# Grouped-query attention with a key/value cache: wide scores, block transposes on VectorE, and an eight-way load of 640 wo rows

## The chip, the cores and the metric

The kernel runs on one core of one Trainium2 chip. The metric is the device time of one execution in microseconds (us), lower is better. TensorE (PE; PEld is its weight load), VectorE (DVE), ScalarE (ACT), GpSimd (POOL) and SyncE (SP) run their own instruction queues in order; sixteen DMA engines carry the loads.

## The reference

Batch 8, four query positions, model width 512, 32 query heads over 8 kv heads (four query heads share one), 2048 cached keys, head size 128, all in bf16.

```
q = (x @ wq).reshape(B, Sq, Hq, Dh).transpose(0, 2, 1, 3)
k = repeat(k_cache, 4, axis=1);  v = repeat(v_cache, 4, axis=1)
p = softmax(einsum("bhqd,bhkd->bhqk", q, k) * Dh**-0.5)
o = einsum("bhqk,bhkd->bhqd", p, v)
out = o.transpose(0, 2, 1, 3).reshape(B, Sq, Hq * Dh) @ wo
```

The inputs are 33.6 MB of keys, 33.6 MB of values, 4.2 MB of wq, 4.2 MB of wo and 32 KB of x; the output is 32 KB.

## The kernel before

**Units.** The work is cut into 16 units `(hq, b)`: one batch entry and four kv heads. One unit's keys are one load of 2 MB into a tile of 128 partitions x 64 keys x 128 (32 partitions per kv head), its values another. `kpool` and `vpool` have three buffers each. The projection of x (L164 to L206) is made once, into `q_bd`, which holds the queries in two halves `e` of the head size, zero where the other half stands.

**One unit's steps.** `transpose_part(u, t)` (L143), for t = 0 to 3, turns a quarter of the keys on TensorE, two bf16 at a time as one fp32, through PSUM tiles `kp`; VectorE copies them to `kt`. `scores(u)` (L212) makes 32 matmuls of 256 columns: the 128 rows of `s_ps` are 4 quarters `t` of the keys x 32, and the four kv heads `g` follow each other in the columns. ScalarE takes the exponential head by head (four instructions, each with a sum `l_sb`). `probs_to_keys(u)` (L236) turns the 128x128 blocks of probabilities with 8 TensorE transposes into `pt`, and ScalarE copies the four 32-row bands into `probs`. `norms(u)` (L252) gathers the sums with a matmul against ones and takes the reciprocal; `values(u, half)` (L273) is 32 matmuls a half against the value tile; `finish(u)` scales the result into `oT`.

**The order** is written out by hand (`manual_schedule`, the loop at L323). Iteration n turns the keys of unit n in four parts, and between them makes the scores of unit n-1 and the norms and values of unit n-2. After unit B (half of the heads done), `to_tokens` and `to_wo_rows` (L295, L303) bring the outputs from head order into rows of wo; after the last unit they do it for the other half. `project(p, r0, n)` multiplies by wo: `wo_sb[:, p, r, :]` holds row r of each partition's eight rows of part p, and four parts are summed in `out_ps`.

**The loads** all go through SP's queue in the order of a list: k0, wq, x, k1, then k(u) and v(u-2) in turn; part 0 of wo stands before v14, parts 1 and 2 and four quarters of part 3 come last. `load_ready` issues what the free buffers allow; a load into a buffer that is still read waits at the head of SP's queue. wo takes the place of wq in SBUF (one buffer, tag "w"). Every load but x has 128 partitions as its outermost dimension on both sides; x has 32.

Of the kernel before, what the change touches and what calls it, by code (L numbers as in the profile page):

```python
# [14 lines left out]
def kernel(  # L15
# [18 lines left out]
    G = 4  # L34
# [7 lines left out]
    NP = Hq // HP  # L42
    DH = D // 2
    NU = (Hkv // G) * B
    KB, VB = 3, 3
    scale = float(Dh) ** -0.5
    AX = mybir.AxisListType.X
# [4 lines left out]
    const = ctx.enter_context(tc.tile_pool(name="const", bufs=1))  # L52
# [22 lines left out]
    by_q = const.tile([128, HQ], FP32, name="by_q")  # L75
    oT = [const.tile([128, HP, 2, B, Sq], BF16, name=f"oT{n}") for n in range(2)]
    oP = [const.tile([128, WR, 2, T], BF16, name=f"oP{n}") for n in range(2)]
    nat_sb = const.tile([2 * T, HP * 128], BF16, name="nat_sb")
# [30 lines left out]
    for u in range(2, NU + 2):  # L109
        if u < NU:  # L110
            loads.append(("k", u))
        if u == NU:
            loads.append(("w", 0))
        loads.append(("v", u - 2))
    loads.reverse()

    def load_ready(nk, nv):

        while loads:
            kind, u = loads[-1]  # L120
            if kind == "w":
                load_wo(u, 0, WR)
# [12 lines left out]
    nc.gpsimd.memset(probs[1][:, :, :, :], 0.0)  # L135
    nc.gpsimd.memset(ones[:, :], 1.0)
    nc.vector.tensor_reduce(
        out=by_q[:, :], in_=ident4[:, :].rearrange("p (c q) -> p q c", q=HQ), axis=AX, op=ADD
    )

    kt = {}
# [1 line left out]
    def transpose_part(u, t):  # L143

        k4 = ks[u][:, :, :].rearrange("s c d -> s (c d)").bitcast(FP32)
        kt[(u, t)] = ktpool.tile([128, J, 128, 2], BF16, tag="kt", name="kt")
        for half in range(2):
            kp = psum_k.tile([128, J // 2, 128], FP32, tag="k", name="kp")
            for j in range(J // 2):
                w = (t * J + half * J // 2 + j) * 128  # L150
                nc.tensor.transpose(kp[:, j, :], k4[:, w : w + 128], ident4[:, :])  # L151
            nc.vector.tensor_copy(  # L152
                out=kt[(u, t)][:, half * J // 2 : (half + 1) * J // 2, :, :].rearrange(
                    "k j s e -> k (j s e)"
                ),
                in_=kp[:, :, :].rearrange("k j s -> k (j s)").bitcast(BF16),
            )

# [10 lines left out]
    nc.vector.tensor_copy(out=xT_sb[:, :, :], in_=xtp[:, :, :])  # L169
    q_nats = []  # L170
    for hq in range(Hkv // G):
        psq = psum_s.tile([128, rep * Dh], FP32, tag="s", name="psq")
# [38 lines left out]

    def scores(u):  # L212
        hq, b = units[u]
        s_sbs[u] = small.tile([128, J, G, S], BF16, tag="s_sb", name="s_sb")
        l_sbs[u] = small.tile([128, G], FP32, tag="l_sb", name="l_sb")
        for gg in range(G // 2):
            s_ps = psum_s.tile([128, 2, J, S], FP32, tag="s", name="s_ps")
            for g in range(2 * gg, 2 * gg + 2):
                for e in range(2):
                    for t in range(NT):  # L220
                        nc.tensor.matmul(  # L221
                            s_ps[t * 32 : (t + 1) * 32, g % 2, :, :],
                            lhsT=q_bd[:, hq, e, g, b, :, :],
                            rhs=kt[(u, t)][:, :, g * S : (g + 1) * S, e],
                            start=(e == 0),
                            stop=(e == 1),
                        )
            for g in range(2 * gg, 2 * gg + 2):
                nc.scalar.activation(  # L229
                    out=s_sbs[u][:, :, g, :],  # L230
                    in_=s_ps[:, g % 2, :, :],
                    func=EXP,
                    accum_out=l_sbs[u][:, g : g + 1],
                )

    def probs_to_keys(u):  # L236
        pt = psum_t.tile([128, J, 128], BF16, tag="t", name="pt")
        for j in range(J):
            nc.tensor.transpose(  # L239
                pt[:, j, :], s_sbs[u][:, j, :, :].rearrange("q g s -> q (g s)"), ident[:, :]  # L240
            )
        pr = probs[u % 2]
        for g in range(G):
            rows = slice(g * S, (g + 1) * S)
            nc.scalar.copy(  # L245
                out=pr[rows, :, g, :],
                in_=pt[rows, :, :].rearrange("s j (c q) -> s (j c) q", q=HQ),
            )

    r_sbs = {}  # L250

    def norms(u):  # L252
        by_gq = small.tile([128, G, HQ], FP32, tag="by_gq", name="by_gq")
        nc.vector.tensor_tensor(  # L254
            out=by_gq[:, :, :],
            in0=l_sbs[u][:, :].unsqueeze(2).to_broadcast([128, G, HQ]),
            in1=by_q[:, :].unsqueeze(1).to_broadcast([128, G, HQ]),
            op=MULT,
        )
        l_ps = psum_l.tile([128, NQ], FP32, tag="l", name="l_ps")  # L260
        nc.tensor.matmul(  # L261
            l_ps[:, :],
            lhsT=ones[:, :],
            rhs=by_gq[:, :, :].rearrange("k g q -> k (g q)"),
            start=True,
            stop=True,
        )
        r_sbs[u] = small.tile([128, NQ], FP32, tag="r_sb", name="r_sb")
        nc.vector.reciprocal(r_sbs[u][:, :], l_ps[:, :])  # L269
# [3 lines left out]
    def values(u, half):  # L273
        if half == 0:
            o_pss[u] = psum_o.tile([128, NQ], FP32, tag="o", name="o_ps")
        for i in range(half * C // 2, (half + 1) * C // 2):
            j, t, c = i // 8, i // 2 % 4, i % 2
            nc.tensor.matmul(  # L278
                o_pss[u][:, :],
                lhsT=vs[u][:, 2 * (t * J + j) + c, :],  # L280
                rhs=probs[u % 2][:, i, :, :].rearrange("s g q -> s (g q)"),
                start=(i == 0),
                stop=(i == C - 1),
            )
# [10 lines left out]
    def to_tokens(n):  # L295
        nat = psum_l.tile([2 * T, HP, 128], BF16, tag="l", name="nat")
        for h in range(HP):
            nc.tensor.transpose(
                nat[:, h, :], oT[n][:, h, :, :, :].rearrange("d p b s -> d (p b s)"), ident[:, :]
            )  # L300
        nc.vector.tensor_copy(out=nat_sb[:, :], in_=nat[:, :, :].rearrange("t h d -> t (h d)"))

    def to_wo_rows(n):  # L303
        perm = psum_l.tile([128, WR, 2, T], BF16, tag="l", name="perm")
        by_row = nat_sb[:, :].rearrange("t (q r) -> t r q", r=WR)
        for r in range(WR):
            nc.tensor.transpose(
                perm[:, r, :, :].rearrange("q p t -> q (p t)"), by_row[:, r, :], ident[: 2 * T, : 2 * T]
            )
        nc.vector.tensor_copy(out=oP[n][:, :, :, :], in_=perm[:, :, :, :])  # L310

    def project(p, r0, n):
# [84 lines left out]
```

## Time and profile before

| | |
|---|---|
| time, three runs | 190.15, 190.44, 190.62 us; median 190.44 us |
| profiled execution | the profile gives its span, 188.4 us from the first to the last instruction; the median of the three runs is 2.0 us above that |
| instructions in the span | 5301 |
| busy | PE 140.1 us (74%), PEld 121.5 (65%), DVE 103.5 (55%), ACT 94.4 (50%), POOL 8.2 (4%) |
| read from HBM | 75.53 MB, 401 GB/s over the span |
| TensorE's granted clock, mean | 0.967 |

Busy time is a union of instruction times on an engine. The profile also names, for each idle stretch, what ended it, and follows a chain of such releases back from the last instruction. For each DMA it has packets with their start, duration and size, and the sixteen increments, one per DMA engine, with which a load's semaphore reaches its full count; it does not number the DMA engines.

### The profile page before, as it was taken

What the parts mean: (1) busy time and instruction counts of PE and PEld (TensorE: products, weight loads), DVE (VectorE), ACT (ScalarE), POOL (GpSimd) and SP (SyncE); (2) the same over time, 40 slices, a digit from 0 to 9 for tenths busy, and PEclk for the clock granted to TensorE, in tenths of its full rate; (3) what the DMA queues carried; (4) which work ended last, traced back from release to release, by engine and by line L of the source; (5) the groups of instructions that cost most, each with busy time, mean ns of one, the idle gap of its engine ahead of it and who ended that gap; (6) DMA issues with size and microseconds to landing.
All of it is one profiled execution on the core that took longest, in us unless ns stands there. A gap on an engine that the chain in (4) does not pass through costs nothing.

```text
span 188.4 us, 5301 instructions
## 1 busy us (share of the span) xinstructions
PE 140.1 (74%) x2356; PEld 121.5 (65%) x2356; DVE 103.5 (55%) x189; ACT 94.4 (50%) x200; POOL 8.2 (4%) x11
## 2 busy tenths in 40 slices
PE   0290869797979777777777888879777777776681
PEld 0290357696968766767675878777767677665560
DVE  4082286777776656574747457575747565740120
ACT  2000243958476573646556093919292837468500
POOL 8800000000000000000000000000000000000000
PEclk9999678999999999999999699999999999999997
DMA  6998999999999999999999999999999999999940
GB/s 202 466 445 383 428 421 431 428 411 435 431 402 438 426 431 411 431 435 414 421 438 421 431 418 435 418 424 435 421 418 438 419 428 412 414 445 414 399 184 12
DMA packets 5926, 75.89 MB, mean 403 GB/s; under 512 B 688, under 2 KB 784, under 8 KB 1296
## 3 DMA queue, kind: packets, MB, share of 16 engines
q1 hardware_dynamic: 5856, 75.55, 95.2%
q8 instruction: 18, 0.29, 0.6%
q14 instruction: 4, 0.03, 0.0%
q10 hardware_dynamic: 48, 0.02, 0.0%
HBM read 75.53 MB, written 0.03 MB: 401 GB/s over the span
## 4 chain that ended last, share of the span: by engine, by line
DMA 69%; PE 23%; DVE 4%; ACT 1%; issue 1%; SPq 1%
DMA wo_sb<-in_wo_dram 25%; DMA k_sb<-in_k_cache_dram 21%; DMA v_sb<-in_v_cache_dram 14%; PE kp L151 11%; DMA x_sb<-in_x_dram 9%; PE o_ps L278 4%; PE s_ps L221 3%; DVE kt L152 3%; PE psq L176 2%; PE pt L239 1%; PE l_ps L261 1%; ACT q_bd L201 1%; DVE q_bd L201 0%; ACT q_nat L185 0%; DVE by_gq L254 0%
## 5 line engine op out<-in xcount | busy, mean ns | idle before, releaser
L152 DVE COPY kt<-kp 128x1024 bf16<-128x1024 bf16 x128 | 82.0, 682 | 42.7 <-PE kp L151 42.6
L245 ACT COPY probs<-pt 32x1024 bf16<-32x1024 bf16 x64 | 64.2, 1002 | 58.4 <-PE pt L239 57.2
L151 PE MATMUL kp<-ident,k_sb 128*128 128x128 f32 x512 | 71.5, 286 | 16.9 <-DMA k_sb<-in_k_cache_dram 16.6
L151 PEld LDWEIGHTS kp<-ident,k_sb 128*128 128x128 f32 x512 | 59.0, 148 | 22.3 <-issue 13.2
L278 PE MATMUL o_ps<-probs,v_sb 128*128 128x64 bf16 x1024 | 35.7, 195 | 4.4 <-DMA v_sb<-in_v_cache_dram 4.4
L278 PEld LDWEIGHTS <-v_sb 128*128 128x128 bf16 x1024 | 34.0, 99 | 5.2 <-DMA v_sb<-in_v_cache_dram 5.1
L229 ACT ACTIVATE s_sb<-s_ps 128x256 bf16<-128x256 f32 x64 | 23.6, 383 | 2.2 <-PE s_ps L221 1.9
L221 PE MATMUL s_ps<-kt,q_bd 128*32 128x256 bf16 x512 | 18.6, 286 | 0.0
L261 PE MATMUL l_ps<-by_gq,ones 128*128 128x64 f32 x32 | 6.9, 298 | 15.6 <-DVE by_gq L254 15.6
L261 PEld LDWEIGHTS l_ps<-by_gq,ones 128*128 128x128 f32 x32 | 4.8, 188 | 19.3 <-DVE by_gq L254 17.6
L221 PEld LDWEIGHTS <-q_bd 128*32 128x32 bf16 x512 | 12.7, 97 | 3.7 <-issue 2.6
L269 DVE RECIPROCAL r_sb<-l_ps 128x64 f32<-128x64 f32 x16 | 8.9, 557 | 9.0 <-PE l_ps L261 9.0
L229 ACT ACTIVATION_READ_ACCUMULATOR s_sb<-s_ps 128x1 f32 x64 | 13.2, 206 | 0.0
L288 DVE TENSOR_TENSOR oT<-o_ps,r_sb 128x64 bf16<-128x64 f32 x16 | 3.6, 224 | 16.1 <-PE o_ps L278 16.1
L185 ACT ACTIVATE q_nat<-psq 128x512 bf16<-128x512 f32 x2 | 1.2, 597 | 20.0 <-PE psq L176 20.0
L239 PE MATMUL pt<-ident,s_sb 128*128 128x128 bf16 x128 | 9.8, 219 | 0.3 <-ACT s_sb L229 0.3
L239 PEld LDWEIGHTS <-s_sb 128*128 128x128 bf16 x128 | 8.4, 98 | 0.6 <-ACT s_sb L229 0.5
L315 PE MATMUL out_ps<-wo_sb,oP 128*32 128x256 bf16 x64 | 4.5, 274 | 1.0 <-DMA wo_sb<-in_wo_dram 0.5
L364 ACT CAST out_sb<-out_ps 64x256 bf16<-64x256 f32 x1 | 0.4, 365 | 8.2 <-PE out_ps L315 8.2
L315 PEld LDWEIGHTS <-oP 128*32 128x32 bf16 x64 | 3.0, 96 | 2.0 <-issue 0.9
L176 PE MATMUL psq<-wq_sb,xT_sb 128*32 128x512 bf16 x32 | 3.5, 623 | 0.3 <-DVE xT_sb L169 0.3
L134 POOL MEMSET probs<- 128x4096 bf16 x1 | 3.5, 3511 | 0.0
(27 smaller groups left out, 29.1 us busy)
## 6 DMA issues: line engine op xcount, KB each, us to landing
k_sb<-in_k_cache_dram SPq DMA_DIRECT2D x16, 2048.0 KB, 21.8
v_sb<-in_v_cache_dram SPq DMA_DIRECT2D x16, 2048.0 KB, 25.3
wq_sb<-in_wq_dram SPq DMA_DIRECT2D x1, 4096.0 KB, 17.0
wo_sb<-in_wo_dram SPq DMA_DIRECT2D x3, 1024.0 KB, 23.7
wo_sb<-in_wo_dram SPq DMA_DIRECT2D x4, 256.0 KB, 22.3
x_sb<-in_x_dram SPq DMA_DIRECT2D x1, 32.0 KB, 16.7
out_dram<-out_sb SPq DMA_DIRECT2D x1, 16.0 KB, 1.4
out_dram<-out_sb ACTq DMA_DIRECT2D x1, 16.0 KB, 1.6
```

Of the source, the lines that this page charges most:

```text
L151: nc.tensor.transpose(kp[:, j, :], k4[:, w : w + 128], ident4[:, :])
L152: nc.vector.tensor_copy(out=kt[(u, t)][:, half * J // 2 : (half + 1) * J // 2, :, :].rearrange("k j s e -> k (j s e)"), in_=kp[:, :, :].re ...
L176: nc.tensor.matmul(psq[g * T : (g + 1) * T, :], lhsT=xT_sb[:, r, :], rhs=wq_sb[:, r, c0 : c0 + rep * Dh], start=(r == 0), stop=(r == R - 1),)
L221: nc.tensor.matmul(s_ps[t * 32 : (t + 1) * 32, g % 2, :, :], lhsT=q_bd[:, hq, e, g, b, :, :], rhs=kt[(u, t)][:, :, g * S : (g + 1) * S, e] ...
L229: nc.scalar.activation(out=s_sbs[u][:, :, g, :], in_=s_ps[:, g % 2, :, :], func=EXP, accum_out=l_sbs[u][:, g : g + 1],)
L239: nc.tensor.transpose(pt[:, j, :], s_sbs[u][:, j, :, :].rearrange("q g s -> q (g s)"), ident[:, :])
L245: nc.scalar.copy(out=pr[rows, :, g, :], in_=pt[rows, :, :].rearrange("s j (c q) -> s (j c) q", q=HQ),)
L261: nc.tensor.matmul(l_ps[:, :], lhsT=ones[:, :], rhs=by_gq[:, :, :].rearrange("k g q -> k (g q)"), start=True, stop=True,)
L269: nc.vector.reciprocal(r_sbs[u][:, :], l_ps[:, :])
L278: nc.tensor.matmul(o_pss[u][:, :], lhsT=vs[u][:, 2 * (t * J + j) + c, :], rhs=probs[u % 2][:, i, :, :].rearrange("s g q -> s (g q)"), star ...
L288: nc.vector.tensor_tensor(out=oT[hq][:, :, :, b, :].rearrange("d h p s -> d p h s"), in0=o_pss[u][:, :].rearrange("d (p h s) -> d p h s", ...
L315: nc.tensor.matmul(out_ps[half * T : (half + 1) * T, :], lhsT=oP[p // 2][:, r, p % 2, :], rhs=wo_sb[:, p, r, half * DH : (half + 1) * DH], ...
```

## The change

Six things are changed together.

1. **Scores.** One `s_ps` tile of two PSUM banks for a unit; the 128 rows are now 4 kv heads x 32, and a matmul has 512 columns: 16 matmuls instead of 32. One exponential instruction with one sum replaces four. `kt` holds half of a unit's keys in a tile (three buffers instead of six of half the size).
2. **Probabilities.** The eight TensorE transposes, their PSUM tile and pool go; VectorE turns the scores in 32x32 blocks of 4-byte elements (two bf16 side by side), SBUF to SBUF, and ScalarE's four copies read that tile.
3. **Norms.** A per-partition scalar multiplication replaces the product of two broadcast tensors.
4. **PSUM and SBUF.** `psum_k` has four buffers instead of three, and `psq` moves there. The pool `const` is opened after the pools of the large tiles, and a pad of 384 bytes stands ahead of them: the tiles of wq, wo, k, v and kt now start at multiples of 512 bytes, where they started 192 bytes past one.
5. **wo.** The first 640 rows of part 0 are dealt out so that row `(b * 8 + a) * 5 + r` goes to partition `16 a + b`; they are loaded in two pieces (two and three of the five row slots), after v4 and after v10, with 8 as the source's outermost dimension. The other 384 rows are loaded where all of part 0 was.
6. **The turn into wo rows** follows that deal for half 0 (three copies in `to_tokens`, 16 small matmuls in `to_wo_rows`), and uses matmuls into fp32 in place of transposes into bf16.

```diff
+    XR = 5
...
+    align = ctx.enter_context(tc.tile_pool(name="align", bufs=1))
+    align.tile([128, 192], BF16, name="pad")
...
-    ktpool = ctx.enter_context(tc.tile_pool(name="ktpool", bufs=6))
+    ktpool = ctx.enter_context(tc.tile_pool(name="ktpool", bufs=3))
+    const = ctx.enter_context(tc.tile_pool(name="const", bufs=1))
...
-    psum_k = ctx.enter_context(tc.tile_pool(name="psum_k", bufs=3, space=bass.MemoryType.PSUM))
-    psum_s = ctx.enter_context(tc.tile_pool(name="psum_s", bufs=2, space=bass.MemoryType.PSUM))
-    psum_t = ctx.enter_context(tc.tile_pool(name="psum_t", bufs=1, space=bass.MemoryType.PSUM))
+    psum_k = ctx.enter_context(tc.tile_pool(name="psum_k", bufs=4, space=bass.MemoryType.PSUM))
+    psum_s = ctx.enter_context(tc.tile_pool(name="psum_s", bufs=1, space=bass.MemoryType.PSUM))
...
     def load_wo(p, r0, n):
-        rows = wo[p * HP * 128 : (p + 1) * HP * 128, :].rearrange("(q r) j -> q r j", r=WR)
-        nc.sync.dma_start(wo_sb[:, p, r0 : r0 + n, :], rows[:, r0 : r0 + n, :])
+        rows = wo[p * HP * 128 : (p + 1) * HP * 128, :]
+        if p == 0 and r0 < XR:
+            rows = rows[: 128 * XR, :].rearrange("(b a r) j -> a b r j", a=8, r=XR)
+            nc.sync.dma_start(wo_sb[:, p, r0 : r0 + n, :], rows[:, :, r0 : r0 + n, :])
+        elif p == 0:
...
+            rows = rows[128 * XR :, :].rearrange("(q r) j -> q r j", r=WR - XR)
+            nc.sync.dma_start(wo_sb[:, p, r0:, :], rows)
...
         if u == NU:
-            loads.append(("w", 0))
+            loads.append(("w", (XR, WR - XR)))
         loads.append(("v", u - 2))
+        if u == 6:
+            loads.append(("w", (0, 2)))
+        if u == 12:
+            loads.append(("w", (2, 3)))
...
+        s_ps = psum_s.tile([128, 2, 2 * J, S], FP32, tag="s", name="s_ps")
+        for tp in range(2):
+            for e in range(2):
+                for g in range(G):
+                    nc.tensor.matmul(
+                        s_ps[g * 32 : (g + 1) * 32, tp, :, :],
+                        lhsT=q_bd[:, hq, e, g, b, :, :],
+                        rhs=kt[(u, tp)][:, :, g * S : (g + 1) * S, e],
...
+        nc.scalar.activation(
+            out=s_sbs[u][:, :, :, :].rearrange("q a s j -> q a j s"),
+            in_=s_ps[:, :, :, :].rearrange("q t (a j) s -> q (t a) j s", j=2),
+            func=EXP,
+            accum_out=l_sbs[u][:, :],
+        )
...
-        pt = psum_t.tile([128, J, 128], BF16, tag="t", name="pt")
-        for j in range(J):
-            nc.tensor.transpose(
-                pt[:, j, :], s_sbs[u][:, j, :, :].rearrange("q g s -> q (g s)"), ident[:, :]
-            )
+        p_t = small.tile([128, 2 * J * 2, HQ, 2], BF16, tag="p_t", name="p_t")
+        nc.vector.transpose(
+            p_t[:, :, :, :].rearrange("s x q j -> s (x q j)").bitcast(FP32),
+            s_sbs[u][:, :, :, :].rearrange("q a s j -> q (a s j)").bitcast(FP32),
+        )
...
+        nc.vector.tensor_scalar_mul(
+            out=w_gq[:, :],
+            in0=by_gq[:, :, :].rearrange("k g q -> k (g q)"),
+            scalar1=l_sbs[u][:, 0:1],
+        )
...
-        perm = psum_l.tile([128, WR, 2, T], BF16, tag="l", name="perm")
+        perm = psum_l.tile([128, WR, 2, T], FP32, tag="l", name="perm")
...
+            if n == 0:
+                first = by_few[:, r, :] if r < XR else by_rest[:, r - XR, :]
+                for p, in_ in enumerate([first, by_row[:, r, :]]):
+                    nc.tensor.matmul(
+                        perm[:, r, p, :],
+                        lhsT=in_,
+                        rhs=ident[: 2 * T, p * T : (p + 1) * T],
...
```

More of the change, by code (lines that the diff above doesn't have):

```diff
@@ L50 @@
     assert Dh == 128 and C == 64 and J == 8 and HQ == 16 and NU == 16 and T == 32
-    const = ctx.enter_context(tc.tile_pool(name="const", bufs=1))
+    align = ctx.enter_context(tc.tile_pool(name="align", bufs=1))
+    align.tile([128, 192], BF16, name="pad")
     wpool = ctx.enter_context(tc.tile_pool(name="wpool", bufs=1))
@@ L74 @@
     ones = const.tile([128, 128], FP32, name="ones")
-    by_q = const.tile([128, HQ], FP32, name="by_q")
+    by_gq = const.tile([128, G, HQ], FP32, name="by_gq")
     oT = [const.tile([128, HP, 2, B, Sq], BF16, name=f"oT{n}") for n in range(2)]
@@ L101, in load_wo @@
     def load_wo(p, r0, n):
-        rows = wo[p * HP * 128 : (p + 1) * HP * 128, :].rearrange("(q r) j -> q r j", r=WR)
-        nc.sync.dma_start(wo_sb[:, p, r0 : r0 + n, :], rows[:, r0 : r0 + n, :])
+        rows = wo[p * HP * 128 : (p + 1) * HP * 128, :]
[3 more added lines that the diff above has]
+        elif p == 0:
+            assert (r0, n) == (XR, WR - XR)
+            rows = rows[128 * XR :, :].rearrange("(q r) j -> q r j", r=WR - XR)
+            nc.sync.dma_start(wo_sb[:, p, r0:, :], rows)
+        else:
+            rows = rows.rearrange("(q r) j -> q r j", r=WR)
+            nc.sync.dma_start(wo_sb[:, p, r0 : r0 + n, :], rows[:, r0 : r0 + n, :])
     load_k(0)
@@ L121, in load_ready @@
             if kind == "w":
-                load_wo(u, 0, WR)
+                load_wo(0, *u)
             elif u >= (nk + KB if kind == "k" else nv + VB):
@@ L137 @@
     nc.vector.tensor_reduce(
-        out=by_q[:, :], in_=ident4[:, :].rearrange("p (c q) -> p q c", q=HQ), axis=AX, op=ADD
+        out=by_gq[:, :, :],
+        in_=ident4[:, :].rearrange("p (g c q) -> p g q c", g=G, c=2),
+        axis=AX,
+        op=ADD,
     )
@@ L145, in transpose_part @@
         k4 = ks[u][:, :, :].rearrange("s c d -> s (c d)").bitcast(FP32)
-        kt[(u, t)] = ktpool.tile([128, J, 128, 2], BF16, tag="kt", name="kt")
+        if t % 2 == 0:
+            kt[(u, t // 2)] = ktpool.tile([128, 2 * J, 128, 2], BF16, tag="kt", name="kt")
         for half in range(2):
             kp = psum_k.tile([128, J // 2, 128], FP32, tag="k", name="kp")
+            j0 = (t % 2) * J + half * J // 2
             for j in range(J // 2):
@@ L152, in transpose_part @@
             nc.vector.tensor_copy(
-                out=kt[(u, t)][:, half * J // 2 : (half + 1) * J // 2, :, :].rearrange(
-                    "k j s e -> k (j s e)"
-                ),
+                out=kt[(u, t // 2)][:, j0 : j0 + J // 2, :, :].rearrange("k j s e -> k (j s e)"),
                 in_=kp[:, :, :].rearrange("k j s -> k (j s)").bitcast(BF16),
@@ L171 @@
     for hq in range(Hkv // G):
-        psq = psum_s.tile([128, rep * Dh], FP32, tag="s", name="psq")
+        psq = psum_k.tile([128, rep * Dh], FP32, tag="k", name="psq")
         for r in range(R):
@@ L213, in scores @@
         hq, b = units[u]
[L214 to L226, printed above, removed]
-                        )
[L228 to L234, printed above, removed]
@@ L236, in probs_to_keys @@
-    def probs_to_keys(u):
-        pt = psum_t.tile([128, J, 128], BF16, tag="t", name="pt")
-        for j in range(J):
-            nc.tensor.transpose(
-                pt[:, j, :], s_sbs[u][:, j, :, :].rearrange("q g s -> q (g s)"), ident[:, :]
-            )
+        s_ps = psum_s.tile([128, 2, 2 * J, S], FP32, tag="s", name="s_ps")
[6 more added lines that the diff above has]
+                        rhs=kt[(u, tp)][:, :, g * S : (g + 1) * S, e],
+                        start=(e == 0),
+                        stop=(e == 1),
+                    )
@@ new lines, in scores @@
+        s_sbs[u] = small.tile([128, 2 * J, S, 2], BF16, tag="s_sb", name="s_sb")
+        l_sbs[u] = small.tile([128, 1], FP32, tag="l_sb", name="l_sb")
+        nc.scalar.activation(
[4 more added lines that the diff above has]
+        )
+    def probs_to_keys(u):
+        p_t = small.tile([128, 2 * J * 2, HQ, 2], BF16, tag="p_t", name="p_t")
[3 more added lines that the diff above has]
+        )
@@ L245, in probs_to_keys @@
             nc.scalar.copy(
-                out=pr[rows, :, g, :],
-                in_=pt[rows, :, :].rearrange("s j (c q) -> s (j c) q", q=HQ),
+                out=pr[rows, :, g, :].rearrange("s (x j) q -> s x j q", j=2),
+                in_=p_t[rows, :, :, :].rearrange("s x q j -> s x j q"),
             )
@@ L252, in norms @@
     def norms(u):
[L253 to L258, printed above, removed]
+        w_gq = small.tile([128, NQ], FP32, tag="w_gq", name="w_gq")
+        nc.vector.tensor_scalar_mul(
+            out=w_gq[:, :],
+            in0=by_gq[:, :, :].rearrange("k g q -> k (g q)"),
+            scalar1=l_sbs[u][:, 0:1],
         )
@@ L263, in norms @@
             lhsT=ones[:, :],
-            rhs=by_gq[:, :, :].rearrange("k g q -> k (g q)"),
+            rhs=w_gq[:, :],
             start=True,
@@ L276, in values @@
         for i in range(half * C // 2, (half + 1) * C // 2):
-            j, t, c = i // 8, i // 2 % 4, i % 2
+            a, c, j = i // 4, i // 2 % 2, i % 2
             nc.tensor.matmul(
                 o_pss[u][:, :],
-                lhsT=vs[u][:, 2 * (t * J + j) + c, :],
+                lhsT=vs[u][:, 2 * (2 * a + j) + c, :],
                 rhs=probs[u % 2][:, i, :, :].rearrange("s g q -> s (g q)"),
@@ L300, in to_tokens @@
             )
-        nc.vector.tensor_copy(out=nat_sb[:, :], in_=nat[:, :, :].rearrange("t h d -> t (h d)"))
+        n_cols = nat[:, :, :].rearrange("t h d -> t (h d)")
+        if n == 0:
+            nc.vector.tensor_copy(
+                out=nat_sb[:T, : 128 * XR].rearrange("t (r a b) -> t r a b", r=XR, a=8),
+                in_=n_cols[:T, : 128 * XR].rearrange("t (b a r) -> t r a b", a=8, r=XR),
+            )
+            nc.vector.tensor_copy(out=nat_sb[:T, 128 * XR :], in_=n_cols[:T, 128 * XR :])
+            nc.vector.tensor_copy(out=nat_sb[T:, :], in_=n_cols[T:, :])
+        else:
+            nc.vector.tensor_copy(out=nat_sb[:, :], in_=n_cols)
     def to_wo_rows(n):
-        perm = psum_l.tile([128, WR, 2, T], BF16, tag="l", name="perm")
+        perm = psum_l.tile([128, WR, 2, T], FP32, tag="l", name="perm")
         by_row = nat_sb[:, :].rearrange("t (q r) -> t r q", r=WR)
+        by_few = nat_sb[:, : 128 * XR].rearrange("t (r q) -> t r q", r=XR)
+        by_rest = nat_sb[:, 128 * XR :].rearrange("t (q r) -> t r q", r=WR - XR)
         for r in range(WR):
-            nc.tensor.transpose(
-                perm[:, r, :, :].rearrange("q p t -> q (p t)"), by_row[:, r, :], ident[: 2 * T, : 2 * T]
-            )
+            if n == 0:
+                first = by_few[:, r, :] if r < XR else by_rest[:, r - XR, :]
[4 more added lines that the diff above has]
+                        rhs=ident[: 2 * T, p * T : (p + 1) * T],
+                        start=True,
+                        stop=True,
+                    )
+            else:
+                nc.tensor.matmul(
+                    perm[:, r, :, :].rearrange("q p t -> q (p t)"),
+                    lhsT=by_row[:, r, :],
+                    rhs=ident[: 2 * T, : 2 * T],
+                    start=True,
+                    stop=True,
+                )
         nc.vector.tensor_copy(out=oP[n][:, :, :, :], in_=perm[:, :, :, :])
```

## The prediction

> **What bounds the kernel now.** I read the page first: slices, DMA queues, chain.
>
> ```profile
> PE   0290869797979777777777888879777777776681
> DMA  6998999999999999999999999999999999999940
> q1 hardware_dynamic: 5856, 75.55, 95.2%
> q8 instruction: 18, 0.29, 0.6%
> q14 instruction: 4, 0.03, 0.0%
> DMA 69%; PE 23%; DVE 4%; ACT 1%; issue 1%; SPq 1%
> ```
>
> The DMA engines are busy from the second slice to the last but one; no compute engine is. Then the end of the chain in order of time, and a table by window (columns: us, then PE, PEld, DVE, ACT and POOL busy, clock, DMA share, GB/s):
>
> ```profile
> 138.17 27.46 DMA wo_sb<-in_wo_dram
> 165.65 18.93 DMA wo_sb<-in_wo_dram
> 184.58 0.04 issue
> 184.62 0.41 PE out_ps L315 x4
> ...
> 109.30:119.10 9.80, 8.31 (x149) 7.36 (x146) 6.47 (x13) 6.51 (x14) 0.00 (x0) 1.00 1.00 425
> ```
>
> The stream of loads ends at 184.58; what follows (four matmuls, a cast, the store) lasts 3.8 us and stays. In a unit of 9.8 us DMA is full, PE has 1.5 us to spare, DVE and ACT 3.3. Loads are issued far ahead (median 21.8 us from issue to landing for keys, of which 4.9 is the transfer), so compute has room.
>
> The page doesn't say why the last slices empty unevenly. Each load ends with sixteen increments, one per DMA engine. From the trace:
>
> ```
> load          sixteen increments, us
> k2            27.60 27.63 27.66 27.66 27.67 27.68 27.70 27.75 27.78 27.81 27.82 27.83 27.90 27.91 27.97 28.02
> v0            32.50 32.52 32.55 32.55 32.56 32.58 32.60 32.64 32.68 32.70 32.71 32.72 32.78 32.85 32.90 34.33
> last wo piece 179.68 179.70 179.73 179.81 180.04 180.09 181.12 181.78 182.73 182.76 182.80 182.91 182.92 182.96 184.57 184.58
> ```
>
> Every engine moves 131,072 B of a 2 MB load in 4.895 us (26.8 GB/s) with no gap, all at the same pace; but one fell 1.43 us behind just after an instruction packet (queue q8, 16 KB, 29.9 us). Followed from load to load, all delays are of this kind: a 16 KB instruction packet sets its engine back 1.43 to 1.58 us, an 8 KB one (q14) 0.8 to 1.0. The eighteen large ones go round the same eight engines: six are hit twice (182.73 to 182.96), two three times (184.57, 184.58). The eight others get none; two of those got two small packets each (181.12, 181.78). **The time is that of the DMA engine hit most often.**
>
> **The change, part by part.**
>
> *Fewer PE instructions.* When the q8 packets start, PE has done 261, 545, ..., 4653 instructions: about one packet per 256. Now 2356 matmuls + 2356 weight loads = 4712 (18.4 x 256, 18 packets). Removed: 16 x 16 score matmuls and 128 transposes; added: 8 in the turn of half 0. 1980 x 2 = 3960, 15.5 x 256: 15 packets. Over eight engines that is at most two each: the last engine ends at 182.96 instead of 184.58, **-1.62 us**.
>
> *640 wo rows with outer dimension 8.* They are 655,360 B. Over sixteen engines each carries 40,960 B, 1.53 us; over eight, 81,920 B, 3.06 us. No row shows a load with so short an outer dimension. If all sixteen carry it, nothing moves. If eight do, those gain +1.53 us and the others lose 1.53. Smaller pieces cost little: the 256 KB wo loads, in 2 KB pieces, step by 0.66 us where 16 KB per engine otherwise take 0.61, so at most 0.25 for 80 KB, more likely 0.1. If the carriers are the eight that get no large packets, the engines hit twice end at 182.96 - 1.53 = 181.43, the untouched ones at 180.09 + 1.63 = 181.72, and the one with two small packets at 181.78 + 1.63 = **183.41**: that is last, 0.45 later than without this edit. (DVE's instruction count hardly changes, so its two small packets stay; ACT falls from 238 to about 130 and keeps one.) If carriers and large packets coincide, even in part, the end is 182.96 + 1.63 = 184.59.
>
> [...]
>
> Which eight, the trace doesn't say, as engines are not numbered. For disjoint groups: the packets go round eight engines in a fixed order and spare eight, as many as would carry the load, so a fixed half is hit. Against: in the first load the engines' first packets start in some order (1.76 to 2.97 us), and engines hit later are found early and late in it. I take the disjoint groups, at odds of about two to one.
>
> *Aligned tiles.* Packets: 16 KB 611 to 620 ns, 32 KB 1213, all written 192 B past a multiple of 512. Two of 16 KB against one of 32 KB: 2 x 611 - 1213 = 9 ns per packet is all that can be blamed on its edges. Bounds: 0, and 9 ns x 288 (4.72 MB per engine / 16 KB) = -2.6 us. The 8 KB instruction packets, not written into these tiles, have the same excess (307 to 309 ns); I take 0.
>
> [...]
>
> *ScalarE.* Four exponentials and reads, 4 x (383 + 206) = 2.36 us per unit, become one of 1024 columns: from 383 (256) and 597 (512), 1.03 + 0.21. The four copies (1002 ns each) now read SBUF in steps of 4 bytes: 0.75 to 1.5 each; I take 1.0. Per unit 5.2, at worst 7.3, of 9.8.
>
> *VectorE* gains a block transpose of 128 x 512 four-byte elements: no such row. Between 0.45 (memset, 2048 such in 1765 ns) and 1.4 (two copies of 682); I take 0.6. 6.5 + 0.6 = 7.1, at worst 7.9, of 9.8. It waits for the exponential, which ended 4 us before TensorE's transposes of that unit (132.8 against 136.2); behind it on DVE are `oT` and the next unit's `kt` copies, which PE's key transposes and so k's buffers wait for. *TensorE* loses 0.6 us per unit. All this lies under the DMA stream and costs nothing; were a unit to need 10.0 us, the cover would go at 0.2 us x 14 = +2.8.
>
> *SP's queue* gets two issues more (0.33 to 0.94 us) ahead of loads that have some 15 us to spare: nothing. *The turn of half 1*, after v15: v15 lands 7.6 us before the stream's end, the path from it (177.04) to the last-but-two project (183.71) is 6.7; the copy from fp32 takes 0.69 (the `q_nat` row) for 0.42. Covered with 0.6 to spare. Half 0's extra copies lie mid-stream.
>
> **Sum.** 183.41 - 184.58 = -1.2 us; the span goes to 187.2, and with the 2.0 between span and median the time to **189.2 us**.
>
> **The rivals.**
> 1. *The load spreads over all sixteen*, the change of wo does nothing: 182.96, 188.8 us.
> 2. *Starts of tiles do cost*: half to all of 2.6 us goes on top of the forecast: 186.6 to 187.9, say 187.5. For it: every large load starts off the mark. Against: the equal excess above.
> 3. *The carriers include engines with two large packets*: 184.59, 190.4, no change; the scattered start order speaks for it.
> 4. *Slower: the eight carriers collide where they write.* All large loads of before cut their 128 partitions over the sixteen engines in the same way; the new ones cut them over eight, so a carrier writes into partitions that another engine is streaming to. If two writers halve each other, half of the carriers need 3.06 us more: 180.09 + 1.63 + 3.06 = 184.8 (190.7 us), or, with two large packets, 187.65 (193.5). It decides as soon as the extra passes 1.2 us, at once in case 3. [...] Against: x's 1 KB packets, whose 32 partitions are also cut differently, all took 46 ns; but they are short.
> 5. *Compute binds* (above): 193.
>
> [...]
>
> **How the numbers follow.** Forecast 0.36, rival 1 0.06, rival 2 0.18, rival 3 0.20, rival 4 0.15, compute 0.05. Runs of before spread by 0.25%, so about 0.3% (0.57 us) can be told from no change. Faster: 0.36 + 0.06 + 0.18 = 0.60; same: 0.20; slower: 0.20. The range runs from 187.0 (rival 2 but its extreme) to 191.0 (rival 4's mild end); what is left out is the rest of rivals 4 and 5 and rival 2's tip, 0.2.
>
> **What would show it.** Right: q8 with 15 packets; the last load's increments within 2 us, the latest near 183.4; each half-load of wo with eight increments at once; DMA share 0.99 or more in every unit. Wrong: a carrier that falls back far more than 3.1 us over the two pieces (rival 4); a 16 KB packet below 610 ns (rival 2); a last increment at 184.6 on an engine that was hit twice (rival 3); waits of PE for DVE that grow, with a DMA share under 0.97 (compute).

## The result and the profile after

The changed kernel takes **196.58 us** (median of 196.53, 199.88, 196.63 and 196.10) against 190.53 of the kernel before in the same session (190.15 to 190.71): a ratio of 1.0312, 95% interval 1.029 to 1.0335. It is slower by 6.1 us, where 1.2 us faster than 190.44 was forecast. Ratios here leave out runs over 1.5% above their kernel's fastest; medians and listed times hold all runs.

The profiled execution took 196.53 us with a span of 194.8. From its page (slices, DMA queues, share of the chain by engine, groups):

```profile
PE   0291888797777777589768978786777886766672
PEclk9999699799999999889997999999769997996998
DMA  6999999999999999999999999999999999999500
GB/s 212 448 431 421 431 427 427 431 424 431 422 431 427 427 361 382 431 427 431 429 427 431 427 431 427 431 427 285 402 427 431 426 431 413 435 427 410 227 3 8
q8 instruction: 15, 0.25, 0.5%
q14 instruction: 4, 0.03, 0.0%
DMA 59%; PE 23%; ACT 8%; DVE 6%; issue 1%; SPq 0%; ACTq 0%
L261 ACT COPY probs<-p_t 32x1024 bf16<-32x1024 bf16 x64 | 66.7, 1043 | 62.1 <-DVE p_t L254 60.9
L245 ACT ACTIVATE s_sb<-s_ps 128x1024 bf16<-128x1024 f32 x16 | 21.1, 1316 | 3.7 <-PE s_ps L236 3.4
L254 DVE STREAM_TRANSPOSE p_t<-s_sb 128x512 f32<-128x512 f32 x16 | 11.2, 702 | 4.5 <-ACT s_sb L245 4.5
```

Two things differ from the page of before. The DMA engines still count as busy, yet in two places (slices of 4.9 us, at 68 to 78 and 131 to 141 us) they move only 285 to 402 GB/s: these are the two eight-way pieces of wo. And the last slices have no DMA at all: the end has passed from the stream to compute, as ScalarE's 8% and VectorE's 6% of the chain say (1% and 4% before).

The end of the chain of waits, in order of time (start, length, engine, result, line):

```profile
139.11 23.21 DMA k_sb<-in_k_cache_dram
...
162.46 1.65 PE kp L171 x8
...
172.90 1.05 ACT probs L261
...
176.10 1.05 ACT probs L261
177.17 1.31 ACT s_sb L245
...
178.73 0.72 DVE p_t L254
179.47 1.05 ACT probs L261
...
182.68 1.05 ACT probs L261
...
183.77 2.04 PE o_ps L293 x64
...
189.13 1.94 PE out_ps L356 x32
```

Keys 15 can be turned only from 162.46. From 172.90 the path runs over ScalarE, and from one step to the next there is no wait: four copies of unit 14, the exponential of unit 15, the block transpose on VectorE, four copies of unit 15, and only then values(15). v15 had landed at 178.53, so the data waited 5 us for ScalarE. Before, the same spot looked like this (timeline; in brackets what the engine had waited for):

```profile
158.39 1.06 PE L151 MATMUL kp<-ident,k_sb 128*128 128x128 f32 x8 [1.01 <-DMA k_sb<-in_k_cache_dram]
...
172.74 4.08 ACT L245 COPY probs<-pt 32x1024 bf16<-32x1024 bf16 x4 [0.77 <-PE pt L239]
...
177.04 1.14 PE L278 MATMUL o_ps<-probs,v_sb 128*128 128x64 bf16 x33 [1.60 <-DMA v_sb<-in_v_cache_dram]
```

The copies ended at 176.82, v15's landing (176.99) let values(15) start at 177.04: compute was 0.2 us ahead of the stream.

The difference by stages of the end:

| us | before | after | |
|---|---|---|---|
| turn of keys 15 starts | 158.39 | 162.46 | +4.07 |
| from there to values(15) | 18.65 | 21.31 | +2.66 |
| from values(15) to the end of the last project | 7.97 | 7.28 | -0.69 |
| end of the last project | 185.01 | 191.05 | +6.04 |
| last increment of the last wo load | 184.58 | 185.88 | +1.30 |

So there are two questions: why keys 15 come 4 us late, and why lateness is paid in full though the stream itself ends only 1.3 us later. The theories: **C** (collision), the eight-way pieces slow other transfers where they write; **T** (tail), the path from keys 15 through ScalarE's copies to values(15) sets the end; **F** (few), a load on eight engines is slow because of the few carriers, wherever it writes; **A** (alignment), the start of the tiles sets the packets' pace. (The recorded expectations name their theories A, B and so on each for itself.)

### The profile page after: what moved, and what is told of

It is laid out like the page before. It is cut to its first block, busy times and chain, and to the rows that moved or that the text cites. A ratio compares the mean times of both kernels' runs of the same rounds, so it can differ in the third digit from the quotient of the medians.

```text
span 194.8 us, 4459 instructions
## 1 busy us (share of the span) xinstructions
PE 138.9 (71%) x1980; PEld 112.5 (58%) x1980; DVE 113.9 (58%) x207; ACT 96.2 (49%) x104; POOL 8.2 (4%) x11
## 4 chain that ended last, share of the span: by engine, by line
DMA 59%; PE 23%; ACT 8%; DVE 6%; issue 1%; SPq 0%; ACTq 0%
DMA v_sb<-in_v_cache_dram 26%; DMA k_sb<-in_k_cache_dram 24%; PE kp L171 9%; DMA x_sb<-in_x_dram 9%; ACT probs L261 6%; PE o_ps L293 6%; DVE kt L172 4%; PE s_ps L236 3%; PE psq L194 2%; PE out_ps L356 2%; DVE p_t L254 1%; ACT s_sb L245 1%; PE l_ps L276 1%; DVE oP L351 0%; DVE q_bd L219 0%
## 5 line engine op out<-in xcount | busy, mean ns | idle before, releaser
L261 ACT COPY probs<-p_t 32x1024 bf16<-32x1024 bf16 x64 | 66.7, 1043 | 62.1 <-DVE p_t L254 60.9
L171 PE MATMUL kp<-ident,k_sb 128*128 128x128 f32 x512 | 74.4, 295 | 22.9 <-DMA k_sb<-in_k_cache_dram 22.3
L245 ACT ACTIVATE s_sb<-s_ps 128x1024 bf16<-128x1024 f32 x16 | 21.1, 1316 | 3.7 <-PE s_ps L236 3.4
L236 PE MATMUL s_ps<-kt,q_bd 128*32 128x512 bf16 x256 | 19.9, 433 | 0.0
L276 PE MATMUL l_ps<-w_gq,ones 128*128 128x64 f32 x32 | 6.9, 297 | 16.3 <-DVE w_gq L270 16.3
L276 PEld LDWEIGHTS l_ps<-w_gq,ones 128*128 128x128 f32 x32 | 4.8, 188 | 20.3 <-DVE w_gq L270 15.7
L254 DVE STREAM_TRANSPOSE p_t<-s_sb 128x512 f32<-128x512 f32 x16 | 11.2, 702 | 4.5 <-ACT s_sb L245 4.5
L203 ACT ACTIVATE q_nat<-psq 128x512 bf16<-128x512 f32 x2 | 1.2, 597 | 19.8 <-PE psq L194 19.8
L236 PEld LDWEIGHTS <-q_bd 128*32 128x32 bf16 x256 | 5.7, 101 | 7.7 <-issue 5.0
L270 DVE TENSOR_SCALAR w_gq<-by_gq,l_sb 128x64 f32<-128x64 f32 x16 | 3.9, 244 | 0.0
L149 POOL MEMSET probs<- 128x4096 bf16 x1 | 3.5, 3511 | 0.0
L150 POOL MEMSET probs<- 128x4096 bf16 x1 | 3.5, 3511 | 0.0
```

Source lines behind the costliest of these rows:

```text
L236: nc.tensor.matmul(s_ps[g * 32 : (g + 1) * 32, tp, :, :], lhsT=q_bd[:, hq, e, g, b, :, :], rhs=kt[(u, tp)][:, :, g * S : (g + 1) * S, e], ...
L245: nc.scalar.activation(out=s_sbs[u][:, :, :, :].rearrange("q a s j -> q a j s"), in_=s_ps[:, :, :, :].rearrange("q t (a j) s -> q (t a) j ...
L254: nc.vector.transpose(p_t[:, :, :, :].rearrange("s x q j -> s (x q j)").bitcast(FP32), s_sbs[u][:, :, :, :].rearrange("q a s j -> q (a s j ...
L261: nc.scalar.copy(out=pr[rows, :, g, :].rearrange("s (x j) q -> s x j q", j=2), in_=p_t[rows, :, :, :].rearrange("s x q j -> s x j q"),)
L270: nc.vector.tensor_scalar_mul(out=w_gq[:, :], in0=by_gq[:, :, :].rearrange("k g q -> k (g q)"), scalar1=l_sbs[u][:, 0:1],)
L276: nc.tensor.matmul(l_ps[:, :], lhsT=ones[:, :], rhs=w_gq[:, :], start=True, stop=True,)
```

## The experiments

**The same early pieces, dealt over all 128 partitions as usual** (sixteen engines carry them).

```diff
-rows = rows[: 128 * XR, :].rearrange("(b a r) j -> a b r j", a=8, r=XR)
+rows = rows[: 128 * XR, :].rearrange("(q r) j -> q r j", r=XR)
 # nat_sb is dealt to match: "t (q r) -> t r q"
```

> The changed kernel with the same two early pieces of wo, the same 640 rows, at the same places in the load order, but dealt so that 128 partitions are the outermost dimension on both sides. Theory A (the eight carriers collide with the other engines where they write): the 16 KB packets around the pieces go back from up to 1.0 us to 0.61, the pieces' own from 149 and 192 ns to 84 and 121, the stream of loads ends near 181 instead of 185.9, keys 15 land near 157.5 instead of 162.3, and since the chain from keys 15 to values(15) took 21.4 us and TensorE was throttled in it, the time falls to 190 to 192. Theory B (the whole loss is the longer compute chain after the last keys, the eight-way pieces cost nothing): the stream still ends near 185.9 and the time stays at 195 to 197.

Measured: 195.64 (193.25 to 196.77), ratio 1.0236 (1.017 to 1.0303). The windows of the two pieces (us, then PE, PEld, DVE, ACT and POOL busy, clock, DMA share, GB/s), of after, with a window without a piece between them:

```profile
69.00:78.00 9.00, 6.65 (x110) 5.22 (x108) 6.36 (x12) 4.22 (x5) 0.00 (x0) 1.00 1.01 360
86.00:95.00 9.00, 7.65 (x121) 6.47 (x120) 6.96 (x13) 4.66 (x5) 0.00 (x0) 1.00 1.01 433
131.00:140.00 9.00, 7.17 (x98) 6.29 (x90) 5.01 (x10) 2.83 (x4) 0.00 (x0) 0.81 1.03 340
```

and of this run, with a window in its tail:

```profile
69.00:78.00 9.00, 6.52 (x110) 5.32 (x108) 6.49 (x12) 4.88 (x6) 0.00 (x0) 1.00 1.00 424
131.00:140.00 9.00, 5.16 (x91) 4.84 (x90) 5.19 (x10) 5.19 (x7) 0.00 (x0) 0.94 1.02 432
173.00:183.00 10.00, 8.49 (x125) 7.30 (x122) 1.88 (x5) 4.77 (x6) 0.00 (x0) 0.50 0.67 273
```

The steps of its end:

```profile
158.90 1.06 PE kp L171 x8
...
178.69 3.59 PE o_ps L293 x64
...
185.88 1.94 PE out_ps L356 x32
```

At an equal DMA share of 1.0 the bytes fall by a fifth in after and not here: the engines are occupied, but stretched. The stream ends at 181.65 instead of 185.88 (-4.2) and keys 15 are turned from 158.90 (-3.6). The profiled run is the fastest of the four, 193.25, and lies 3.3 us under after's profiled 196.53: keys 15 come 3.6 us earlier, the path from them to values(15) is 1.5 shorter (19.8 for 21.3), and from values(15) to the last project it is 1.8 longer (9.11 for 7.28), with TensorE at a granted clock of 0.50. The other three runs (195.51 to 196.77) left no trace, so why the median falls by only 0.9 is not shown. C is right on the stream; but even the fastest run misses the 190 to 192 that C was expected to give: keys 15 land at 158.57, not near 157.5, and the half clock costs the 1.8. The path through ScalarE's copies still sets the end, as T says: the last project ends at 187.8, 6.1 us behind the stream.

**The shifted tiles alone** (in the kernel before).

```diff
-const = ctx.enter_context(tc.tile_pool(name="const", bufs=1))
+align = ctx.enter_context(tc.tile_pool(name="align", bufs=1))
+align.tile([128, 192], BF16, name="pad")
 ...
+const = ctx.enter_context(tc.tile_pool(name="const", bufs=1))  # after ktpool
```

> The kernel before with one edit: the pad and the later opening of the pool const, so that the tiles of wq, wo, k, v and kt start at multiples of 512 bytes. Theory A (a misaligned start costs every packet some 7 ns): 16 KB packets all take 611 ns, a load steps by 4.84 us instead of 4.895, the stream ends near 182.6 and the time is 188.5. Theory B (the faster pace seen in the changed kernel comes from something else): 4.895 and 190.5.

Measured: 192.23, 188.56, 194.75, 189.68, 191.30, 191.35 and 190.81; ratio 0.9998 (0.9952 to 1.0043). Neither expectation holds as it stands. The best run is 1.8 us below before, but the profiled one (192.23) shows on its page

```profile
GB/s 196 465 441 389 382 365 379 379 372 379 427 432 430 429 420 430 423 434 430 437 423 423 423 434 437 427 423 434 420 434 437 423 418 434 422 437 422 406 216 13
```

from the fourth to the tenth slice (14 to 48 us) 365 to 389 GB/s. In the trace a 16 KB packet takes 700 ns from about 18 to 47 us, after that 611. 29 us at 0.70 us a packet are 41 packets, and 41 x 89 ns = 3.7 us is just what separates this run from the 188.56. After the stretch the loads follow each other mostly at 4.84 to 4.86 us, where before has 4.88 to 4.91. So A holds outside the stretch, and in this run a second effect outweighs it. The other six runs left no trace; whether the same effect keeps their median at that of before is not shown.

**The eight-way pieces alone** (in the kernel before, with the turn into wo rows that belongs to them).

```diff
+if p == 0 and r0 < XR:
+    rows = rows[: 128 * XR, :].rearrange("(b a r) j -> a b r j", a=8, r=XR)
 ...
+if u == 6:  loads.append(("w", (0, 2)))
+if u == 12: loads.append(("w", (2, 3)))
```

> The kernel before with the eight-way load of 640 wo rows alone, and the turn into wo rows that goes with it. Theory A (the carriers collide): the stream of loads ends 3 to 5 us later, 193.5 to 195.5 us. Theory B (the eight-way pieces are harmless, or help to balance the engines): 189.5 to 191.

Measured: 198.21 (197.68 to 198.98), ratio 1.0417 (1.0384 to 1.0449). The same windows as above:

```profile
69.00:78.00 9.00, 7.61 (x138) 6.54 (x136) 5.92 (x11) 4.51 (x12) 0.00 (x0) 1.00 1.01 353
131.00:140.00 9.00, 5.87 (x95) 5.00 (x96) 4.90 (x9) 3.66 (x11) 0.00 (x0) 1.00 1.03 304
```

Without any other part of the change, the pieces cost 7.9 us (198.21 - 190.32 of that session), more than the whole change, and more than either theory allowed. Keys 15 are turned from 166.02 (+7.6), while the stream ends 4.6 later, as C expected. 1.53 us of that lateness is no collision: 655,360 B now travel ahead of keys 15 instead of behind them.

**The change without the pad.**

```diff
-align.tile([128, 192], BF16, name="pad")
+const = ctx.enter_context(tc.tile_pool(name="const", bufs=1))  # opened first, as before
```

> The changed kernel without the pad and with const opened first, so that the large tiles start off the 512-byte mark again. Theory A (alignment is worth 0.055 us per 2 MB load): keys 15 land some 1.8 us later, the time is near 198.4. Theory B (alignment is worth nothing): 196.5.

Measured: 198.84 (197.78 to 199.84), ratio 1.0446 (1.0397 to 1.0494): 2.3 us above the change. In this kernel the alignment helps, about as much as a step of 4.84 us per 2 MB instead of 4.895 gives over 36 such loads (-2.0).

**wo's first part whole and late, as before, the rest of the change kept.**

```diff
-    loads.append(("w", (XR, WR - XR)))
+    loads.append(("w", 0))
-if u == 6:  loads.append(("w", (0, 2)))
-if u == 12: loads.append(("w", (2, 3)))
```

> The changed kernel with part 0 of wo loaded whole, where the kernel before has it (no early pieces, no deal). Theory A (the eight-way pieces cost the stream about 4 us, and the rest of the loss is the chain from keys 15 through ScalarE's copies to values(15), about 20 us at full clock): the stream ends near 181, keys 15 are turned from about 157.3, values(15) start near 177 although v15 is there near 173.5, the last project ends 7.3 (full clock) to 9.1 us (half clock) later; 189.5 to 192 us, still bound by the tail and not by the stream. Theory C (with the pieces gone the stream bounds the end again, and the fewer instruction packets and the alignment show in full): 181 + 3.8 + 2.0 = 186.8 us.

Measured, ten times: 192.77, 190.35, 189.65, 194.69, 190.94, 189.23, 190.74, 194.53, 191.03, 196.75; median 190.99, ratio 1.0004 (0.9978 to 1.003). 5.6 us of the loss are gone with the early pieces. The profiled run (192.77) again has a slow stretch, packets of 681 ns from 18 to 53 us; the three longer ones left no trace.

**The change with half the copies of the last two units on VectorE.**

```diff
-nc.scalar.copy(
+(nc.vector.tensor_copy if u >= NU - 2 and g % 2 else nc.scalar.copy)(
```

> The changed kernel with one edit in its tail: for the last two units two of the four copies of the probabilities go to VectorE, which is idle then. Everything before is as in the changed kernel. Theory A (the copies on ScalarE after keys 15 set the end): copies 14 and 15 take about 2.3 us each instead of 4.2, values(15) start about 3.5 to 4 us earlier (near 180), 192 to 193.5 us instead of 196.5. Theory B (the lost time is in the stream alone): 196 to 197.

Measured: 191.42, 193.70, 193.73 and 191.44, ratio 1.0115 (1.005 to 1.0179), 4.0 us below the change in the median. The end of its chain:

```profile
174.61 0.72 DVE p_t L254
175.43 0.68 DVE probs L261
176.12 0.69 DVE probs L261
...
178.69 1.99 PE o_ps L293 x64
```

Keys 15 are turned at 162.04, as late as in after, but values(15) start at 178.7 instead of 183.77. From keys 15 to values(15) it takes 16.65 us. Against the 19.8 of the first experiment, where the clock was full at that point as it is here, the shared copies save about 3.1; some 1.5 more of the difference from after is its half clock on leaving the wait for keys 15 (see below). T is shown: the copies are not hidden at the end.

**Both.** wo whole and late, and the shared copies.

> Both: part 0 of wo whole, and the copies of the last two units shared by ScalarE and VectorE. Theory A: stream near 181, values(15) near 173.5 to 174.5 with v15, the end within 1 to 2 us of the stream's: 187 to 189 us, less than both kernels. Theory B (alignment brings the longer packets that one of the runs showed for 28 us): 189 to 192 with a spread of several us.

Measured: 187.15, 191.44, 187.15, 190.56. In the two shorter runs the repairs together give 9.4 us, nearly the sum of what they give alone (5.6 and 4.0). In the profiled run, one of 187.15, the stream, which ends at 181.60, binds again; keys 15 are turned from 157.22. The two long runs left no trace; with four runs so far apart the gain over before (190.25) is not settled.

**Idle time and the clock.** The first experiment with 40 extra transposes, 24 ahead of values(14) and 16 behind the first project, ahead of values(15); nobody reads them.

```diff
+def warm(count):  # transposes of ks[NU - 1] into a psum_k tile
 ...
+if n == NU + 1: project(0, 0, WR); warm(16)
+if n == NU: warm(24)
```

> The changed kernel with the two early pieces dealt over 128 partitions (as in the first experiment, 195.6 us), and 40 extra key transposes on TensorE, whose results nothing reads, put where it waits for the last copies of probabilities. Theory D (TensorE's granted clock halves when it idles in the tail, and the half clock lengthens the last 9 us): the granted clock stays 1.0 from 173 on, values(15) to the last project takes 7.3 instead of 9.1 us, the time falls by 1.5 to 2.5 us to 193 to 194. Theory E (the half clock has no part in it): no change or up to 0.5 us more.

Measured: 195.67 (194.93 to 197.61), ratio 1.0293 (1.0237 to 1.035): the time doesn't fall. The window of its tail, to be set beside the 0.50 above:

```profile
173.00:183.00 10.00, 7.82 (x146) 7.03 (x145) 1.53 (x4) 8.03 (x9) 0.00 (x0) 1.00 0.93 381
```

and the two steps to be set beside those of the first experiment:

```profile
182.02 2.04 PE o_ps L293 x64
...
187.39 1.94 PE out_ps L356 x32
```

The clock stays at 1.00, and from values(15) to the last project it takes 7.29 us instead of 9.11. But a stretch of 681 ns packets (18 to 53 us) made keys 15 3.3 us later in this run than in the first experiment's, so the time proves nothing; only the trace shows the 1.8 us. One of the other runs (197.61) had a mean granted clock of 0.758, the lowest on record here, and left no trace: that extra transposes keep the clock up is shown for one execution only.

**Is it the few carriers, or the place?** The version with both repairs and three extra loads of 327,680 B that nobody reads: into the lower 64 partitions on eight engines, into the upper 64 on eight, into the upper 64 on sixteen.

```diff
+loads.append(("x", {5: (0, 8), 8: (64, 8), 11: (64, 64)}[u]))  # first partition, outer dimension
```

> The version with wo whole and shared copies (187.15 to 191.4 us), with three extra loads of 64 wo rows x 5 into a tile that nothing reads, 327,680 B each: after v3 into partitions 0 to 63 with outer dimension 8, after v6 into partitions 64 to 127 with outer dimension 8, after v9 into partitions 64 to 127 with outer dimension 64. Theory A (writes collide on paths that belong to partitions): the first collides only among its own carriers, so few 16 KB packets of keys and values go over 640 ns; the second meets the engines that stream to the upper half, so some 30 to 60 of them do, up to 1.2 us; the third, though all sixteen engines carry it, meets them too. Theory F (it is the number of carriers: eight engines get more bytes and fall behind, with no collision): 16 KB packets stay at 611 ns in all three places, and the first and second look alike.

Measured: 198.90 (one run). A window without an extra load, then the three with one:

```profile
50.00:60.00 10.00, 7.95 (x130) 6.38 (x131) 7.37 (x16) 7.52 (x8) 0.00 (x0) 1.00 1.01 430
59.00:68.00 9.00, 6.82 (x112) 5.39 (x109) 6.33 (x12) 4.86 (x6) 0.00 (x0) 1.00 1.01 359
93.00:102.00 9.00, 4.87 (x88) 4.26 (x86) 5.20 (x10) 3.08 (x4) 0.00 (x0) 1.00 1.01 263
124.00:133.00 9.00, 5.50 (x76) 4.26 (x77) 5.03 (x9) 5.57 (x6) 0.00 (x0) 1.00 1.01 288
```

And the packets in flight while each was moved, from the trace (a 5 KB packet alone takes 196 ns, a 16 KB one 611):

```
extra load                  5 KB, mean   16 KB packets over 640 ns   longest
lower half, 8 carriers      310 ns       52 of 72                    1416 ns
upper half, 8 carriers      409 ns       63 of 79                    1634 ns
upper half, 16 carriers     303 ns       95 of 133                   1202 ns
```

The third load uses all sixteen engines and hurts as the others do, whereas the first experiment's pieces, also on sixteen but over all 128 partitions, hurt nothing. In the first load, too, it is not only the carriers: in its 4.45 us the other eight engines alone would have passed some 58 packets at 611 ns (an estimate, 8 x 4.45 / 0.611), and only 20 of the 72 are at or under 640. F falls: engines that carry nothing of a load are stretched by it, and few carriers are not needed for that. What fits all the loads is that a transfer which cuts the partitions over the engines in another way than the stream does writes where other engines are writing; the trace doesn't show which engine writes which partition, so this stays an inference. The expectation for the lower half, that few packets would go over 640 ns, failed. Why that half is milder stays open.

**The repaired version without the pad.**

```diff
-align.tile([128, 192], BF16, name="pad")  # const opened first; wo whole; copies shared
```

> The version with wo whole and shared copies, without the pad (large tiles 192 bytes past the 512-byte mark, as in the kernel before). If the stream bounds the end and alignment is worth 2 us of it: 182.96 + 3.8 + 2.0 = 188.8 us, against 187.15 with the pad in its undisturbed runs; if the long stretches of 680 to 700 ns packets belong to the aligned starts, the spread over the runs is below 1 us here; if they do not, it is several us here too.

Measured: 188.42, 188.56, 189.93, 188.54, 188.55, 188.61; median 188.55 against 190.44, ratio 0.9919 (0.9893 to 0.9946). **It beats both kernels.** The end of its chain:

```profile
137.58 27.96 DMA wo_sb<-in_wo_dram
165.56 17.30 DMA wo_sb<-in_wo_dram
...
182.90 0.41 PE out_ps L318 x4
```

The stream sets the end again. Its last increments (us):

```
179.53 179.68 179.74 179.84 179.97 180.24 180.35 181.26 181.85 182.21 182.66 182.69 182.71 182.74 182.83 182.86
```

The latest is 182.86, where 182.96 was worked out for engines hit by two large instruction packets; the page counts 15 of them, and no engine ends where those hit three times did (184.57). The spread over the runs is 1.5 us, not below 1 as expected, by the one run of 189.93; the other five lie within 0.2.

**The kernel before with the shared copies.**

```diff
-nc.scalar.copy(
+(nc.vector.tensor_copy if u >= NU - 2 and g % 2 else nc.scalar.copy)(
```

> The kernel before with the copies of the last two units shared by ScalarE and VectorE, nothing else. Theory A (in the kernel before the stream of loads sets the end, with v15 landing 0.2 us after the last copy of probabilities): no change, 190.0 to 190.6 us. If the tail were the bound already: 187 to 188.

Measured: 192.23 (191.57 to 194.00), ratio 1.0112 (1.0072 to 1.0152): a miss. Its timeline in unit 15:

```profile
173.09 1.00 ACT L245 COPY probs<-pt 32x1024 bf16<-32x1024 bf16 x1 [2.40 <-PE pt L239]
174.19 0.68 DVE L245 COPY probs<-pt 32x1024 bf16<-32x1024 bf16 x1 [2.90 <-ACT probs L245]
174.91 1.00 ACT L245 COPY probs<-pt 32x1024 bf16<-32x1024 bf16 x1 [0.82 <-DVE probs L245]
175.94 0.70 DVE L245 COPY probs<-pt 32x1024 bf16<-32x1024 bf16 x1 [1.07 <-ACT probs L245]
177.07 0.43 PE L261 MATMUL l_ps<-by_gq,ones 128*128 128x64 f32 x2 [2.36 <-DVE by_gq L254]
```

Out of the PSUM tile `pt` the two engines copy in turns, each waiting for the other, so that four copies still take 3.55 us (4.08 on ScalarE alone), and VectorE's `by_gq` of the last unit now queues behind its copies, with TensorE behind that: values(15) start at 178.54 instead of 177.04. From the SBUF tile `p_t` of the changed kernel they copy side by side: four copies in 2.1 us. So the run doesn't test whether before is bound by the stream alone; it shows how little delay its tail bears. Why the turns arise was not tried.

## Why the prediction was wrong, point by point

**Right: the stream and instruction packets.** 15 large packets were forecast and came; with the early pieces and the tail repaired, the stream ends within 0.1 us of the place worked out. The gain of 1.6 us is real: in the repaired version without the pad the stream ends 1.7 us earlier than in before (184.58 - 182.86), and the time is 1.9 shorter (190.44 - 188.55).

**Right: eight carriers.** That eight engines carry such a load was the author's assumption; no load of before shows it. In after each eight-way load shows one semaphore update as it is issued (50.69 and 111.48 us) and then eight landings (73.18 to 75.26; 134.92 to 137.69), against sixteen elsewhere; rival 1 falls.

**Wrong: the term for wo, +1.63 on the carriers and -1.53 on the others.** The step "smaller pieces cost little" priced each packet as if alone. In after a 2 KB packet takes 84 ns alone, but 123 in the mean of the first piece, and the 16 KB packets streaming beside it are stretched: 59 of 208 between 68 and 78 us lie over 640 ns, the longest at 1236; 65 of 186 around the second piece (132 to 142 us). By the first experiment this costs the stream 4.2 us. This is rival 4, given 0.15, with 3.06 us as its price. What was held against it, x's packets at 46 ns, was the wrong row: they were short and early. The half loads agree with rival 4: sixteen engines into half the partitions stretch other packets as eight do (95 of 133 over 640 ns, against 52 of 72 and 63 of 79). Which engine writes which partition, and what the writers share, no trace shows.

**Wrong: "All this lies under the DMA stream and costs nothing".** This is the step that turned a late stream into a slow kernel. The durations were near enough: the exponential 1316 ns and 0.2 (1.03 and 0.21 were estimated), the copies 1043 (1.0), the transpose 702 (0.6), on ScalarE 5.7 us a unit where 5.2 was forecast and 7.3 the worst; and in mid-stream all is hidden (433 GB/s between the pieces). (One row was misread: the exponential ended 3.4 us ahead of TensorE's transposes, 132.8 against 136.2, not 4; nothing hangs on it.) But the path of the end was followed only from v15 (6.7 us, 0.6 to spare). The one from keys 15, through the copies of units 14 and 15 in a row on ScalarE, was left out; the trace of before showed its last copy ending only 0.2 us ahead of v15's landing. Two additions made it last:
- It starts later. Keys 15 slip by 4.07 us: +1.53 for the bytes now ahead of them, +3.56 for the collisions (162.46 - 158.90), and the rest, -1.0, goes with the better pace.
- It is longer. In the first experiment, with the clock full at that point, the path takes 19.8 us where before took 18.65: about 1.1 us of structure, since the block transpose on VectorE waits behind the `kt` copies before ScalarE can begin its copies (8.9 us after keys 15; 7.9 in before). In after it takes 21.3: TensorE came out of its wait for keys 15 at a granted clock of 0.5 (162.8 to 166.2 us), some 1.5 us by the difference.

**Wrong: alignment taken as 0.** The equal excess of the small instruction packets was no sound argument; with the shifted tiles the loads follow each other at 4.81 to 4.83 us in the early stream (first increments 22.27, 27.10, 31.91, 36.74), where before has 4.89 to 4.90. The shifted tiles were worth 2.3 us between the change with and without the pad, and 1.3 between the ends of the stream in the two repaired versions (182.86 and 181.60). What in the start of a tile costs the time is not shown. This is rival 2, in its effect; the sign named for it, a 16 KB packet below 610 ns, did not come (611 with the pad, 611 to 620 without): the gain shows in the steps between loads. In after it was lost under the rest, and in other versions partly in the slow stretches.

**Open.** Rival 3, whether the eight carriers include engines hit by large packets, can't be read: the collisions scatter the last increments of after from 180.30 to 185.88, far over the 2 us expected. Rival 5, that compute binds, was wrong in mid-stream and right at the end.

## What to carry to other kernels

In a full stream of loads, deal every transfer over the partitions as the stream itself is dealt: here a small one dealt otherwise delayed the stream by more than twice the time of its own bytes (4.2 us for 1.53). Where the stream seems to hide compute, follow every path of the last unit, from its first input too, and note by how much each is behind; with 0.2 us of slack, work moved ahead of that input and work added after it are both paid in full. When a repair moves the median little, read the stages of its profile before dropping it: the first experiment's median fell by 0.9 us, its profiled run by 3.3.

## What the runs showed of the hardware that was not expected

- TensorE's granted clock was 0.5 in some stretches of 3.4 us or a few times that: in after from 162.8, just behind a wait of 2.0 us, in the first experiment from 173.0 to 183.2. From values(15) to the last project it took 9.11 us at 0.50 and 7.29 with extra transposes. Waiting alone doesn't decide it: in before TensorE waited 1.6 us ahead of 177.04, and its clock stayed at 1.00.
- Streams with shifted tiles fall, in some runs, into a slower pace: 680 to 700 ns for a 16 KB packet instead of 611, from about 18 to 47 or 53 us. It was in three of eight profiles with the pad, in none of five without it (before and four versions), too few to say that the pad brings it. Its cause is open. It cost 3.7 us in one of them, so that what the pad gave (1.3 and 2.3 us, above) is no safe gain, and the steadier of the two repaired versions is the one without.
- Copies on ScalarE and VectorE out of one PSUM tile went in turns, four in 3.55 us; out of one SBUF tile they went side by side, four in 2.1 us. The trace shows that each waited for the other, not why.
